# Attention, DFT mixing and feed-forward in one kernel: keys laid out per query tile, totals in bf16, the DFT tail added from PSUM

## The chip, the core and the metric

One core of one Trainium2 chip runs the whole program. The metric is the time of one execution on the device in microseconds (us). Five engines work side by side, each through its own list of instructions in a fixed order: PE (TensorE, matrix products), DVE (VectorE), ACT (ScalarE), POOL (GpSimd) and SP, which here only starts DMAs. They wait for each other by semaphores. PE takes its operands from SBUF and leaves products in PSUM, of which the kernel uses banks of 512 fp32 columns.

## What is computed

```python
# x: 8 batches x (32 global + 512 local rows) x 512, made by attention:
s_g   = scale * q_g @ k_all.T ;  out_g = softmax(s_g) @ v_all          # global queries see all 544 keys
s_ll  = where(|i - j| <= 32, scale * q_l @ k_l.T, -1e9)                # local: a band of 65 keys
s_lg  = scale * q_l @ k_g.T                                            # and all 32 global keys
out_l = softmax([s_lg, s_ll]) @ [v_g; v_l]                             # 8 heads of 64
X = real(fft(fft(x, axis=rows), axis=columns));  u = x + X             # mixing
un = (u - mean) / sqrt(var + 1e-6)                                     # rows of u
out = u + relu(un @ w_ch1) @ w_ch2                                     # 512 -> 2048 -> 512
```

All inputs are fp32. The kernel holds every matrix operand as two fp16 parts (hi and lo) and sums three products, hi by hi, hi by lo, lo by hi.

## The kernel before

**Attention.** Heads are taken in 32 pairs, four per batch; a pair's two heads lie on the lower and upper 64 of the 128 rows, so that their matmuls use half the rows each. The 512 local queries of a pair make four tiles of 128, in an order (`row_order`, L79) chosen for the DFT; the keys are in an order of their own (`key_order`, L84): 15 local keys, the 32 global ones, then all the rest, 559 columns with the doubled 15. Tile j needs 192 consecutive columns from 128j on, and the global ones. `scores` (L610) does two tiles: for each it makes a 192-column product and then a second one, of 64 columns in tile 0 (which takes keys of the far end) and of the 32 global ones in tiles 1 to 3, each in three hi/lo products for two heads. `masked` (L626, DVE) adds the mask and finds the row maximum `nm`; `exps` (ACT) takes the exponential; `p_hi` (ACT) and `p_lo` (POOL, L648) split it into fp16 parts; `turn` transposes it by DMA; `values` (L659) multiplies by the values (`vN` in key order, `vB` a shifted copy made by `v_out`'s DMAs), and `norm` divides. `g_scores`, `g_max`, `g_exp`, `g_values` do the same for the global queries of two pairs at once, `g_scores` as one 512-column and one 32-column product.

**Scales.** So that fp16 parts suffice, arrays are scaled by powers of two taken from sums of squares: ACT's `sums` (L528) leaves one column of partial sums per array, and a matmul with a constant matrix (`total`, L463; `w_norm`, L445, for the weights) adds them over the 128 partitions and spreads the result. Constant `part` and sums are fp32. `z_total` serves two pairs, `dft_scale` a batch.

**Mixing and feed-forward.** Per batch, `d_even` and `d_odd` (DVE, POOL) fold rows of X, `d_first` and `d_second` (L914, L949) are the matrix products of the DFT, `d_add`, `d_addc` (L966, L975) add the results into X. The 32 global rows of a batch go through `d_tailsec` and then `d_as` (ACT, PSUM to `asm`) and `d_tadd` (DVE: two additions from `asm`, L986 and L987, and two multiply-adds from PSUM, L989). Layer norm (`l_bn` to `l_lo`, with `l_un` L1027 and `l_lo` L1037) makes the two fp16 parts of a chunk of 256 rows; `l_turn` transposes by DMA, for chunk 0 `l_flip` (PE) and `l_put` (L1057 on DVE, L1059 on ACT) do it. `f_first` (L1085, `ps<-uh,wh`) and `f_second` (L1104, `acc<-wh,h`) are the feed-forward of 13 chunks; four more are done in two pairs by a scheme with fewer products (L1236, L1303). The weights are scaled and split at the start (`w_lo`, L472, DVE: `wh`).

**The order.** No queue decides at run time. Class `Plan` (L157) gets every step as a job (`jobs_*`) with its engine, a declared duration in us, what it reads and writes, and in some cases a due time; `targets` spreads due times backwards, and `run` places the jobs one after another on each engine by what is ready and what is due first, using the declared durations, margins (`PEM`: extra time asked between an input and PE) and buffer rings. The result is each engine's fixed list. Feed-forward jobs come last in rank and fill PE's gaps. So a changed duration or constant can reorder anything.

Of the kernel before, what the change touches and what calls it, by code (L numbers as in the profile page):

```python
# [20 lines left out]
P = 128  # L21
# [28 lines left out]
L_HOLD = 77.65  # L50
QUEUE = 1.933
LOOK_BY = 31.266
LN, LN1, LN2 = 41.656, 17.202, 49.261
# [5 lines left out]
APER = 103.0  # L59
PL = 34.52  # L60
T_AT, T_PACE = 799.979, 10.217
BOOST = 34.224
BOOST0 = 82.708
# [12 lines left out]
KW = 576  # L76
# [7 lines left out]
def key_order():  # L84
    a = np.arange
    return np.concatenate([a(433, 448), a(32), a(32, 544)])


def shape_constants():
# [23 lines left out]
    q, key = row_order().reshape(4, P, 1), key_order()  # L113
    for n in range(4):
        k = np.full(192, 9999)
        k[:min(192, 559 - P * n)] = key[P * n:P * n + 192]
        g = np.full(32, -1)
        k = np.concatenate([k, key[384:448]]) if n == 0 else np.concatenate([k, g, g])
        if n == 0:
            k[15:47] = -1  # L120
        m[:, n] = np.where((k[None, :] < 0) | (np.abs(q[n] - k[None, :]) <= 32), 0, 0xF149)
# [190 lines left out]
class Kern:  # L312
    def __init__(self, tc, stack, ins, out):
# [9 lines left out]
        self.part = c.tile([P, P], F32, name="part")  # L323
        nc.gpsimd.memset(self.part, 2.0 ** -13)
        self.partb = c.tile([P, P], BF16, name="partb")
        nc.gpsimd.memset(self.partb, 2.0 ** -8)
        self.kT = [c.tile([P, 1152], F16, name=f"kT{i}") for i in range(NKB)]
# [6 lines left out]
        self.junk = c.tile([P, 640], F16, name="junk")  # L334
# [17 lines left out]
        self.pg = c.tile([P, 544], F32, name="pg")  # L352
# [10 lines left out]
        nc.vector.memset(self.pgr, 0.0)  # L363
        self.wb = ep(name="wb", bufs=1)
# [79 lines left out]
    def w_norm(self, k, c):  # L444
        self.nc.tensor.matmul(self.wl[k, c][:, P:P + 1], self.part, self.mx2[:, 4 * k + c:4 * k + c + 1], start=True, stop=True)  # L445
# [61 lines left out]
    def load(self, p):  # L507
        s = self.state(p)
        qk = self.p2.tile([P, SL + 559], F32, name="qk", bufs=3)
        s["q"], s["k"] = qk[:, 0:SL], qk[:, SL:]  # L510
        self.nc.sync.dma_start(qk, self.qk[s["b"], s["hp"]])
# [83 lines left out]
    def prep_hi(self, p, nm):  # L595
# [4 lines left out]
        else:  # L600
            t = [s["kT"][:, KW * a:KW * a + 559] for a in range(2)]
# [8 lines left out]
    def scores(self, i):  # L610
# [76 lines left out]
    def g_scores(self, g):  # L687
        nc, G = self.nc, self.G[g]
        G["sg"] = S = [self.bank(("bank", "Sg", g, o)) for o in range(2)]
        for m, (a, c) in enumerate(((0, 0), (0, 1), (1, 0))):  # L690
            for o in range(2):
                for i in range(2):
                    st = self.st[2 * g + i]
                    qg = self.g[st["b"]]["T"][:, a, st["hp"], 0:64]
                    k = st["kT"][:, KW * c + 527:KW * c + 559] if o else st["kT"][:, KW * c + 15:KW * c + 527]
                    nc.tensor.matmul(S[o][64 * i:64 * i + 64, 0:k.shape[1]], qg, k, start=m == 0, stop=m == 2)  # L696

    def g_max(self, g):
# [12 lines left out]
    def g_hi(self, g):
        self.nc.scalar.activation(self.pgr[:, 0, 15:559], self.pg, AF.Copy)

    def g_lo(self, g):
        self.nc.gpsimd.tensor_sub(self.pgr[:, 1, 15:559], self.pg, self.pgr[:, 0, 15:559])
# [5 lines left out]
    def g_values(self, g):  # L721
# [3 lines left out]
        for c in range(5):  # L725
            n = P if c < 4 else 64
# [250 lines left out]
    def d_as(self, b):  # L977
        d = self.D[b]
        d["asm"] = asm = self.p1.tile([P, NL], F32, name="asm")
        eo = lambda t: t.rearrange("p (o m) -> p o m", o=2)  # L980
        self.nc.scalar.activation(asm[96:P].rearrange("p (m o) -> p o m", o=2), eo(self.d_psum_of(b, 2, 0)[64:96, 0:NL]), AF.Copy, scale=self.dsc[b][1][64:96])
# [776 lines left out]
```

## Time and profile before

| | us |
|---|---|
| median of 3 runs (lowest, highest) | 1017.65 (1015.54, 1017.81) |
| the profiled execution, its own time | 1017.34 |
| its span (first to last recorded instruction) | 1015.5 |
| PE busy (share of the span) | 924.4 (91%) |
| DVE busy | 732.5 (72%) |
| ACT busy | 627.9 (62%) |
| POOL busy | 582.0 (57%) |

The profile is one execution. An engine is busy while one of its compute instructions runs; a matmul's recorded duration includes its way through the array, so that matmuls in a row overlap, and what one costs is read from the distance between starts. Idle time before an instruction is given with the instruction of another engine that ended it (its releaser). "Granted clock" is the share of PE's full clock (2.4 GHz) in a stretch; it is near 1 or at 0.5.

### The profile page before, as it was taken

The page shows a single profiled execution, that of the slowest core. Times are in us where ns is not written, and L with a number is a line of the kernel's source. Part 1 is how long each engine was busy: PE and PEld are TensorE (multiplying, and loading weights), DVE is VectorE, ACT ScalarE, POOL GpSimd, SP SyncE. Part 2 cuts the span into 40 slices and gives each one's busy share as a digit, 9 for nine tenths or more (in the row PEclk, how much of TensorE's full clock was granted, in tenths as well). Part 3 has the DMA queues.
Part 4 walks back from the last instruction along what each step waited for, and adds up shares of the span by engine and source line. Part 5 has one row for each costly group of instructions (what it writes and reads, how often), then busy time and mean ns, then how long its engine had stood idle before and what let it go on. Part 6 is the DMA issues. An engine that isn't in the chain of part 4 may idle for free.

```text
span 1015.5 us, 25506 instructions
## 1 busy us (share of the span) xinstructions
PE 924.4 (91%) x9864; PEld 653.2 (64%) x9864; DVE 732.5 (72%) x1912; ACT 627.9 (62%) x1361; POOL 582.0 (57%) x861
## 2 busy tenths in 40 slices
PE   2555589999999999999999999999999999999996
PEld 1344466766676667677777767777777766666663
DVE  3687898888858977895688788767865665854543
ACT  6996778976796678758685776764653344411210
POOL 5797378675595469558646864692664097920000
PEclk9655579999999999999999999999999999999998
DMA  9899359635675486458636562843371142201001
GB/s 365 278 223 197 126 118 167 105 109 105 130 152 103 83 146 141 113 96 147 156 77 131 104 161 57 151 101 80 59 131 22 25 94 48 48 1 43 1 1 42
DMA packets 225974, 112.62 MB, mean 111 GB/s; under 512 B 200860, under 2 KB 208444, under 8 KB 225852
## 3 DMA queue, kind: packets, MB, share of 16 engines
q1 hardware_dynamic: 225852, 110.99, 49.8%
q8 instruction: 77, 1.26, 0.5%
q14 instruction: 45, 0.37, 0.1%
HBM read 47.40 MB, written 9.44 MB: 56 GB/s over the span
## 4 chain that ended last, share of the span: by engine, by line
PE 73%; DVE 8%; ACT 2%; issue 1%; POOL 0%; DVEq 0%; ACTq 0%; POOLq 0%
PE ps L1085 23%; PE acc L1104 22%; PE bk L1236 7%; PE ps L1303 4%; PE acc L1303 4%; PE bk L624 3%; PE bk L669 2%; PE bk L672 2%; PE bk L949 1%; PE bk L914 1%; DVE pe L632 1%; PE bk L696 1%; DVE xt L986 1%; PE bk L732 1%; DVE h L1094 1%
## 5 line engine op out<-in xcount | busy, mean ns | idle before, releaser
L1104 PE MATMUL acc<-wh,h 128*128 128x512 f16 x1248 | 287.5, 380 | 5.5 <-DVE h L1094 3.4
L1085 PE MATMUL ps<-uh,wh 128*128 128x256 f16 x2496 | 291.9, 274 | 0.2 <-DVE h L1094 0.2
L1085 PEld LDWEIGHTS <-wh 128*128 128x128 f16 x2496 | 241.5, 99 | 35.9 <-issue 0.9
L1104 PEld LDWEIGHTS <-h 128*128 128x128 f16 x1248 | 117.6, 98 | 133.8 <-DVE h L1094 4.3
L648 POOL TENSOR_TENSOR ph<-pe,ph 128x448 f16<-128x448 f32 (+1 forms) x128 | 141.6, 1116 | 75.8 <-ACT ph L643 57.4
L1094 DVE SCALAR_TENSOR_TENSOR h<-ps,h 128x512 f16<-128x512 f32 x104 | 71.6, 688 | 100.9 <-ACT h L1090 99.2
L1090 ACT ACTIVATE h<-ps 128x512 f16<-128x512 f32 x104 | 61.7, 594 | 117.6 <-PE ps L1085 114.8
L639 ACT ACTIVATE pe<-pe,nm 128x224 f32<-128x224 f32 (+1 forms) x256 | 107.0, 475 | 32.0 <-DVE nm L632 31.6
L632 DVE CUSTOM_DVE_ANT_0 pe<-bk,msk,z 128x224 f32<-128x224 f32 (+1 forms) x256 | 102.3, 453 | 10.3 <-PE bk L624 10.0
L643 ACT ACTIVATE ph<-pe 128x448 f16<-128x448 f32 (+1 forms) x128 | 72.8, 582 | 5.4 <-DMA pl<-ph 1.3
L669 PE MATMUL bk<-vN,pl 128*128 128x65 f16 x768 | 67.7, 200 | 5.7 <-DMA pl<-ph 5.5
L669 PEld LDWEIGHTS <-pl 128*128 128x128 f16 x768 | 59.3, 102 | 12.9 <-DMA pl<-ph 6.6
L624 PEld LDWEIGHTS <-qT 64*128 64x128 f16 x1536 | 51.1, 99 | 14.2 <-issue 10.8
L624 PE MATMUL bk<-kT,qT 64*128 64x192 f16 (+2 forms) x1536 | 57.9, 222 | 2.6 <-DVE X L685 0.8
L672 PEld LDWEIGHTS <-pl 96*128 96x128 f16 (+1 forms) x768 | 56.7, 102 | 4.4 <-issue 0.3
L1065 POOL TENSOR_TENSOR ve<-ve 128x2 f32<-128x2 f32 x17 | 9.4, 555 | 85.3 <-DVE unh L1037 35.0
L572 POOL TENSOR_TENSOR vf<-vf,z 128x640 f32<-128x640 f32 x32 | 41.6, 1300 | 28.7 <-DVE ge L534 14.7
L439 PE MATMUL wl<-wm 128*128 128x128 bf16 x128 | 18.2, 288 | 43.7 <-DVE wm L429 42.1
L583 POOL TENSOR_TENSOR vN<-vf,vN 128x640 f16<-128x640 f32 x32 | 45.4, 1417 | 13.1 <-ACT vN L579 12.8
L608 POOL TENSOR_TENSOR kT<-qk,kT 128x559 f16<-128x559 f32 x32 | 41.3, 1290 | 17.7 <-ACT kT L603 14.7
L672 PE MATMUL bk<-vB,pl 96*128 96x65 f16 (+1 forms) x576 | 51.2, 199 | 0.0
L1285 ACT ACTIVATE hb<-ph 128x512 f16<-128x512 f32 x16 | 10.1, 630 | 65.3 <-DVE ph L1270 65.3
(266 smaller groups left out, 1895.3 us busy)
## 6 DMA issues: line engine op xcount, KB each, us to landing
qk<-in_qk SPq DMA_DIRECT2D x32, 535.5 KB
rw<-in_moe_w_ch SPq DMA_DIRECT2D x22, 512.0 KB
vf<-in_v SPq DMA_DIRECT2D x32, 320.0 KB
out<-X SPq DMA_DIRECT2D x13, 512.0 KB
raw<-in_moe_w_ch SPq DMA_DIRECT2D x10, 512.0 KB
vB<-vN SPq DMA_DIRECT2D x32, 97.5 KB
vB<-vN SPq DMA_DIRECT2D x64, 32.5 KB
pl<-ph SPq DMA_TRANSPOSE x128
```

The costliest lines, as they stand in the source:

```text
L624: nc.tensor.matmul(S[h][:, t + w0:t + w1], qT[r, a, j], kT[r, k0:k0 + w1 - w0], start=m == 0, stop=m == 2)
L632: nc.vector.tensor_tensor_reduce(self.per[j][:, h, 0:w], S[h][:, t:t + w], self.msk[:, j, 0:w], z[:, 8:9], 3e38, op0=ALU.add, op1=ALU.min, ...
L639: self.nc.scalar.activation(pe[:, h], pe[:, h], AF.Exp, bias=nm[:, h:h + 1], scale=-1.0)
L643: self.nc.scalar.activation(ph[:, 0, :, 0:WIDE[i % 4]], self.per[i % 4][:, :, 0:WIDE[i % 4]], AF.Copy)
L648: self.nc.gpsimd.tensor_sub(ph[:, 1, :, 0:w], self.per[i % 4][:, :, 0:w], ph[:, 0, :, 0:w])
L669: nc.tensor.matmul(pv[:, j % 2, h], pl[:, 4 * a + 2 * h], vN[:, j, c, h, :], start=m == 0, stop=False)
L672: nc.tensor.matmul(pv[:, j % 2, h], pl[0:n, 4 * a + 2 * h + 1], vb, start=False, stop=m == 2)
L1085: nc.tensor.matmul(ps[:, q], wt[:, w, c0:c0 + P], uh[:, :, 4 * a + kt, :], start=n == 0, stop=n == 11)
L1094: self.nc.vector.scalar_tensor_tensor(h[:, 1], self.fps.pop((c, fp)), 0.0, h[:, 0], op0=ALU.max, op1=ALU.subtract)
L1104: nc.tensor.matmul(self.acc_f[c][j], h[:, a, q, j * P:(j + 1) * P], self.w[1, f][:, w, :], start=f == 0 and a == 0 and w == 0, stop=f == 1 ...
L1236: nc.tensor.matmul(ps, w[x], a[:, :, k * y + o + kt, :], start=m == 0, stop=m == 5)
L1303: nc.tensor.matmul(self.acc_f[c][j], h[:, a, q, j * P:(j + 1) * P], self.w[1, f][:, w, :], start=first and q + a + w == 0, stop=last and q ...
```

## The change

Keys. `key_order` repeats the 32 global keys in front of the key blocks: 655 columns in place of 559. From column 160j - 32 on (`key_at`), tiles 1 to 3 find the 32 global keys and their 192 local ones side by side, and `scores` makes one 224-column product of them; tile 0 keeps 192 + 64. The mask, the values' order (`vB` now has the global values in front, with four DMAs where there were three) and the global queries follow: `g_scores` skips the repeated columns with products of 113, 384 and 47 columns, 18 matmuls where there were 12. A pair's key load grows from 559 to 655 columns beside the 512 of q.

Totals. `total` and `w_norm` read the upper 16 bits of the fp32 sums as bf16, against a bf16 constant `parth`.

DFT tail. `d_as` and the two additions of `d_tadd` go; in their place `d_tadd` makes two more multiply-adds from PSUM.

Plan. Most declared durations and constants are replaced by other numbers; the feed-forward's products are the same.

```diff
 def key_order():
     a = np.arange
-    return np.concatenate([a(433, 448), a(32), a(32, 544)])
+    g = a(32)
+    return np.concatenate([a(433, 448), g, a(32, 241), g, a(241, 369), g, a(369, 497), g, a(497, 544)])
+
+def key_at(j):
+    return 160 * j - 32 if j else 0
...
-PEM, PEM0, SPM = 0.737, 0.718, 0.205
+PEM, PEM0, SPM = 0.944, 0.753, 0.179
...
     def w_norm(self, k, c):
-        ... self.part, self.mx2[:, 4 * k + c:4 * k + c + 1], start=True, stop=True)
+        ... self.parth, self.upper(self.mx2[:, 4 * k + c:4 * k + c + 1]), start=True, stop=True)
...
+    def upper(self, a):
+        return a.bitcast(BF16).rearrange("p (n t) -> p n t", t=2)[:, :, 1]
+
     def total(self, a, o):
         pb = self.bank(o)[:, 0:a.shape[1]]
-        self.nc.tensor.matmul(pb, self.part, a, start=True, stop=True)
+        self.nc.tensor.matmul(pb, self.parth, self.upper(a), start=True, stop=True)
...
-        nc.sync.dma_start(vB[0:64], vN[0:64, 1:4])
-        nc.sync.dma_start(vB[64:96, 1:3], vN[64:96, 4:5].to_broadcast([SG, 2, 2, 2, 65]))
+        nc.sync.dma_start(vB[32:96, 1:3], vN[0:64, 2:4])
+        nc.sync.dma_start(vB[0:32, 1:3], vN[0:32, 4:5].to_broadcast([SG, 2, 2, 2, 65]))
+        nc.sync.dma_start(vB[0:64, 0], vN[0:64, 1])
         nc.sync.dma_start(vB[64:P, 0], vN[0:64, 3])
...
     def scores(...):
-            for o in range(2):
+            for k0, w0, w1 in ((key_at(j), 0, 224),) if j else ((0, 0, 192), (key_at(3), 192, 256)):
                 for m, (a, c) in enumerate(((0, 0), (0, 1), (1, 0))):
-                    k0 = KW * c + (P * j, 384 if j == 0 else 15)[o]
-                    w0, w1 = ((0, 192), (192, WIDE[j]))[o]
                     for h in range(2):
                         r = slice(64 * h, 64 * h + 64)
-                        nc.tensor.matmul(S[h][:, t + w0:t + w1], qT[r, a, j], kT[r, k0:k0 + w1 - w0], start=m == 0, stop=m == 2)
+                        nc.tensor.matmul(S[h][:, t + w0:t + w1], qT[r, a, j], kT[r, KW * c + k0:KW * c + k0 + w1 - w0], start=m == 0, stop=m == 2)
...
     def g_scores(self, g):
-        for m, (a, c) in enumerate(((0, 0), (0, 1), (1, 0))):
-            for o in range(2):
+        for o, at, n in ((0, 0, 113), (0, 113, 384), (1, 0, 47)):
+            for m, (a, c) in enumerate(((0, 0), (0, 1), (1, 0))):
...
-    def d_as(self, b):
-        d = self.D[b]
-        d["asm"] = asm = self.p1.tile([P, NL], F32, name="asm")
-        ...  # ACT copies the even and odd halves out of PSUM
     def d_tadd(self, b):
-        ve, d = self.nc.vector, self.D[b]
-        x, a = d["xt"][96:P], d["asm"][96:P]
-        ve.tensor_add(x[:, 0:256], x[:, 0:256], a[:, 0:256])
-        ve.tensor_add(x[:, 511:255:-1], x[:, 511:255:-1], a[:, 1:257])
-        for (v, t), c in zip(self.pieces(x, self.d_psum_of(b, 2, 1)[96:P]), (self.dsc[b][4], self.dsc[b][3])):
-            ve.scalar_tensor_tensor(v, t, c[96:P], v, op0=ALU.mult, op1=ALU.add)
+        _, inv, _, c0, c1 = self.dsc[b]
+        x, ps = self.D[b]["xt"][96:P], self.d_psum_of(b, 2, 1)
+        for r, k in ((64, (inv, inv)), (96, (c1, c0))):
+            for (v, t), c in zip(self.pieces(x, ps[r:r + 32]), k):
+                self.nc.vector.scalar_tensor_tensor(v, t, c[96:P], v, op0=ALU.mult, op1=ALU.add)
...
-            add("PE", .25, self.z_total, g, r=[acc], w=[zt], margin=PEM if b else PEM0)
+            add("PE", .1, self.z_total, g, r=[acc], w=[zt], margin=PEM if b else PEM0)
...
-            add("PE", rate * .76, self.scores, 2 * p + h, ...)
+            add("PE", rate * (.61 if h else .65), self.scores, 2 * p + h, ...)
...
-                add("ACT", .42, self.d_as, b, r=[pb[0], dsc], w=[("asm", b)], **late)
-                add("DVE", 1.85, self.d_tadd, b, r=[pb[0], dsc, ("asm", b)], w=[("xta", b)], k=[xt], **late)
+                add("DVE", 1.60, self.d_tadd, b, r=[pb[0], dsc], w=[("xta", b)], k=[xt], **late)
```

What this moves on the engines' lists is shown at three places. A row is a line of the code, the instruction, what it writes and reads and its shape; an x and a number at the end stand for that many in a row.

On PE, inside the first score block of pair 4 (the first pair of batch 1): the end of a tile's wide products and the beginning of what follows. `bk_...` are the two PSUM banks of the two heads, kT and qT the keys and queries. The kernel before:

```order
L624 LDWEIGHTS qT
L624 MATMUL bk_123<-kT_63,qT 128x192
L624 LDWEIGHTS qT
L624 MATMUL bk_125<-kT_63,qT 128x192
L624 LDWEIGHTS qT
L624 MATMUL bk_123<-kT_63,qT 128x32
L624 LDWEIGHTS qT
L624 MATMUL bk_125<-kT_63,qT 128x32
```

The changed kernel, at the end of tile 0 and the beginning of tile 1:

```order
L632 LDWEIGHTS qT
L632 MATMUL bk_122<-kT_61,qT 128x64
L632 LDWEIGHTS qT
L632 MATMUL bk_124<-kT_61,qT 128x64
L632 LDWEIGHTS qT
L632 MATMUL bk_122<-kT_61,qT 128x224
L632 LDWEIGHTS qT
L632 MATMUL bk_124<-kT_61,qT 128x224
```

Before, every tile ends with matmuls of 32 columns (64 in tile 0); in the changed kernel tile 1 is 224-column matmuls alone.

On DVE, at the end of batch 0's attention: L429 and L435 work on the weights, L685 and L693 end a pair's `norm`, L831 and L841 begin `d_even`, L632 and L640 are `masked` (one row for the masked block, one for the row maximum). The kernel before:

```order
L684 RECIPROCAL dn<-dn 128x4
L685 TENSOR_TENSOR X<-bk_125,dn 128x2x128
L429 SCALAR_TENSOR_TENSOR wm<-ps_1269,lw 128x512
L831 TENSOR_TENSOR e_1307<-X 128x4x127
L832 COPY e_1307<-X 128x4
L835 TENSOR_TENSOR e_1307<-e_1307 128x2x128
L836 TENSOR_TENSOR e_1307<-e_1307 128x128
L837 TENSOR_TENSOR e_1307<-e_1307 128x128
L632 ISA pe,nm<-bk_122,msk,z 128x224
L632 ISA nm 128x1
L632 ISA pe,nm<-bk_123,msk,z 128x224
L632 ISA nm 128x1
```

The changed kernel:

```order
L640 ISA nm 128x1
L640 ISA pe,nm<-bk_124,msk,z 128x224
L640 ISA nm 128x1
L691 TENSOR_SCALAR dn<-bk_123,z 128x4
L692 RECIPROCAL dn<-dn 128x4
L693 TENSOR_TENSOR X<-bk_123,dn 128x2x128
L481 SCALAR_TENSOR_TENSOR wh<-wm,wsc,wh 128x512
L750 TENSOR_SCALAR dng<-bk_122,z 128x1
L751 RECIPROCAL dng<-dng 128x1
L752 TENSOR_SCALAR xg<-bk_122,dng 128x64
L435 SCALAR_TENSOR_TENSOR wm<-ps_1246,lw 128x512
L841 TENSOR_TENSOR e_1281<-X 128x4x127
```

Before, the first half of `d_even` (five rows) stands ahead of the last two masked units of the batch; in the changed kernel the masked units, the norm and the global rows come first.

On DVE again, between `l_lo` and `l_put` of chunk 0, the last steps ahead of the first feed-forward matmul; L975 and L985 are `d_addc`, L966 and L976 `d_add`, L1057 and L1060 `l_put`. The kernel before:

```order
L1037 TENSOR_TENSOR unh<-un,unh 128x512 x2
L975 SCALAR_TENSOR_TENSOR X<-bk_123,dsc,X 128x2x128 x4
L1057 COPY uh<-bk_125 128x512
L966 SCALAR_TENSOR_TENSOR X<-bk_124,dsc,X 128x2x128 x2
L1057 COPY uh<-flt 128x512
L966 SCALAR_TENSOR_TENSOR X<-bk_124,dsc,X 128x2x128 x2
```

The changed kernel:

```order
L1040 TENSOR_TENSOR unh<-un,unh 128x512 x2
L640 ISA pe,nm<-bk_122,msk,z 128x256
L640 ISA nm 128x1
L640 ISA pe,nm<-bk_124,msk,z 128x256
L640 ISA nm 128x1
L640 ISA pe,nm<-bk_122,msk,z 128x224
L640 ISA nm 128x1
L640 ISA pe,nm<-bk_124,msk,z 128x224
L640 ISA nm 128x1
L985 SCALAR_TENSOR_TENSOR X<-bk_121,dsc,X 128x2x128 x4
L976 SCALAR_TENSOR_TENSOR X<-bk_123,dsc,X 128x2x128 x2
L1060 COPY uh<-bk_122 128x512
```

Four masked blocks of pair 4 now stand between the two, and the bank that `l_put` reads is the one that two of them have read.

## Rows read from the trace of the kernel before

**Rows 1.** What PE waited for, 175 to 1015 us: total, times, longest.

```profile
PE acc L1104 <- DVE h L1094: 3.4, 2, 1.8
PE bk L914 <- DVE z L934: 1.7, 1, 1.7
PE bk L463 <- ACT junk L528: 1.4, 1, 1.4
PE bk L624 <- DVE nm L632: 0.8, 1, 0.8
...
PE bk L463 <- DVE xt L989: 0.5, 1, 0.5
```

**Rows 2.** PE's timeline, 118 to 140 us: start, duration, instruction, count [idle before].

```profile
133.92 4.87 PE L1085 MATMUL ps<-uh,wh 128*128 128x256 f16 x24
```

**Rows 3.** PE's timeline, 454.5 to 461.3 us.

```profile
455.01 2.75 PE L1104 MATMUL acc<-wh,h 128*128 128x512 f16 x12
457.60 2.78 PE L1085 MATMUL ps<-uh,wh 128*128 128x256 f16 x24
460.31 0.82 PE L624 MATMUL bk<-kT,qT 64*128 64x192 f16 x24
461.06 0.20 PE L669 MATMUL bk<-vN,pl 128*128 128x65 f16 x1
461.10 0.20 PE L672 MATMUL bk<-vB,pl 96*128 96x65 f16 x1
```

**Rows 4.** PE's timeline entered inside that score block, at its thirteenth matmul.

```profile
460.65 0.48 PE L624 MATMUL bk<-kT,qT 64*128 64x192 f16 x12
```

**Rows 5.** PE's timeline, 440 to 466 us, in the DFT's second product.

```profile
446.83 0.23 PE L951 MATMUL bk<-altr,zr 64*32 64x129 f16 x1
446.99 0.53 PE L949 MATMUL bk<-c2r,z 128*32 128x129 f16 x9
```

**Rows 6.** PE's timeline, 594.8 to 595.4 us: totals and the next work.

```profile
594.92 0.28 PE L463 MATMUL bk<-vax,part 128*128 128x7 f32 x2
...
595.28 0.38 PE L1085 MATMUL ps<-uh,wh 128*128 128x256 f16 x2
```

**Rows 7.** `d_tadd` by line: durations in ns (least/median/most), first and last start.

```profile
L986 DVE TENSOR_TENSOR xt<-xt,asm x8: 421/422/4840, 146.3 to 802.5; 32x256 f32<-32x256 f32 x8
...
L989 DVE SCALAR_TENSOR_TENSOR xt<-bk,dsc,xt x16: 483/490/495, 147.1 to 803.7; 32x256 f32<-32x256 f32 x16
```

**Rows 8.** Timelines of DVE, POOL and ACT, 264 to 278 us.

```profile
266.60 4.84 DVE L986 TENSOR_TENSOR xt<-xt,asm 32x256 f32<-32x256 f32 x1
...
269.01 2.14 POOL L648 TENSOR_TENSOR ph<-pe,ph 128x512 f16<-128x512 f32 x2
...
273.24 0.85 ACT L639 ACTIVATE pe<-pe,nm 128x224 f32<-128x224 f32 x2 [3.61 <-DVE nm L632]
```

**Rows 9.** PE by stretch: window, length, busy (matmuls), granted clock, DMA share, GB/s.

```profile
367.00:370.00 3.00, 3.00 (x32) 0.50 1.07 230
```

**Rows 10.** PE's timeline, 358 to 373 us.

```profile
366.50 1.73 PE L624 MATMUL bk<-kT,qT 64*128 64x192 f16 x24 [0.78 <-DVE nm L632]
368.16 3.82 PE L1085 MATMUL ps<-uh,wh 128*128 128x256 f16 x24
```

**Rows 11.** Timelines of DVE and ACT, 88 to 136 us.

```profile
88.53 0.69 DVE L831 TENSOR_TENSOR e<-X 128x508 f32<-128x508 f32 x1 [0.98 <-DMA X<-xd]
...
129.31 1.33 DVE L1037 TENSOR_TENSOR unh<-un,unh 128x512 f16<-128x512 f32 x2
...
133.28 0.41 DVE L1057 COPY uh<-flt 128x512 f16<-128x512 f16 x1
...
92.97 0.85 ACT L639 ACTIVATE pe<-pe,nm 128x224 f32<-128x224 f32 x2 [4.00 <-DVE nm L632]
...
108.46 0.74 ACT L528 ACTIVATE junk<-vf 128x640 f16<-128x640 f32 x1 [0.55 <-DMA vf<-in_v]
```

**Rows 12.** DVE's timeline, 166 to 173 us.

```profile
166.66 4.99 DVE L472 SCALAR_TENSOR_TENSOR wh<-wm,wsc,wh 128x512 f16<-128x512 f32 x2
```

More of the change, by code (lines that the diff above doesn't have):

```diff
@@ L75 @@
 AT = (0, 256, 0, 224)
-KW = 576
+KW = 672
+NKC = 655
 def row_order():
@@ L113, in shape_constants @@
     q, key = row_order().reshape(4, P, 1), key_order()
+    key = np.where(key < 32, -1, key)
     for n in range(4):
[L115 to L118, printed above, removed]
+        k = np.full(256, 9999)
+        w = 192 if n == 0 else 224
+        v = key[key_at(n):key_at(n) + w]
+        k[:len(v)] = v
         if n == 0:
-            k[15:47] = -1
+            k[192:] = key[key_at(3):key_at(3) + 64]
         m[:, n] = np.where((k[None, :] < 0) | (np.abs(q[n] - k[None, :]) <= 32), 0, 0xF149)
@@ L322, in __init__ @@
         self.consts = ins
[L323 to L327, printed above, removed]
+        self.parth = c.tile([P, P], BF16, name="parth")
+        nc.gpsimd.memset(self.parth, 2.0 ** -13)
+        self.kT = [c.tile([P, 2 * KW], F16, name=f"kT{i}") for i in range(NKB)]
         vN = self.vna = c.tile([P, 2, 1300], F16, name="vN")
@@ L444, in w_norm @@
     def w_norm(self, k, c):
-        self.nc.tensor.matmul(self.wl[k, c][:, P:P + 1], self.part, self.mx2[:, 4 * k + c:4 * k + c + 1], start=True, stop=True)
+        self.nc.tensor.matmul(self.wl[k, c][:, P:P + 1], self.parth, self.upper(self.mx2[:, 4 * k + c:4 * k + c + 1]), start=True, stop=True)
     def w_scale(self, k, c):
@@ L600, in prep_hi @@
         else:
-            t = [s["kT"][:, KW * a:KW * a + 559] for a in range(2)]
+            t = [s["kT"][:, KW * a:KW * a + NKC] for a in range(2)]
         s["n" + nm] = t
@@ L1369, in jobs_pair @@
         hold = L_HOLD if b else 0.0
-        add("SP", .44, self.load, p, w=[qk], svc=1.6, hold=hold, queue=QUEUE if p else None)
-        add("SP", .44, self.load_v, p, w=[vf], svc=1.0, hold=hold, queue=QUEUE if p else None)
+        add("SP", .47, self.load, p, w=[qk], svc=1.6, hold=hold, queue=QUEUE if p else None)
+        add("SP", .56, self.load_v, p, w=[vf], svc=1.0, hold=hold, queue=QUEUE if p else None)
         add("ACT", .72, self.sums, p, "q", r=[qk], w=[acc, q], margin=LDM)
-        add("ACT", .75, self.sums, p, "k", r=[qk], w=[acc, k], margin=LDM)
+        add("ACT", .83, self.sums, p, "k", r=[qk], w=[acc, k], margin=LDM)
         add("ACT", .83, self.sums_v, p, r=[vf], w=[acc], margin=LDM)
@@ L1396, in jobs_scores @@
         for nm, o, d in (("k", k, kT), ("q", q, qT)):
[L1397 to L1399 removed]
+            x = .05 if nm == "k" else 0
+            add("ACT", .63 + x, self.prep_mul, p, nm, r=[z, o, qk], w=[o])
+            add("ACT", .53 + x, self.prep_hi, p, nm, r=[o, qk], w=[d])
+            add("POOL", 1.20 + 3 * x, self.prep_lo, p, nm, r=[o, qk, d], w=[d])
         vN, vB = ("vN", p), ("vB", p)
@@ L1408, in half @@
             S = [("bank", "S", 2 * p + h, o) for o in range(2)]
-            add("PE", rate * .76, self.scores, 2 * p + h, r=[kT, qT], w=S + [("pe", 4 * p + 2 * h + n) for n in range(2)], t=U[2 * h], margin=pem)
+            add("PE", rate * (.61 if h else .65), self.scores, 2 * p + h, r=[kT, qT], w=S + [("pe", 4 * p + 2 * h + n) for n in range(2)], t=U[2 * h], margin=pem)
             for n in range(2):
@@ L1412, in half @@
                 pe, ph = ("pe", u), ("ph", u)
-                add("DVE", .92 if p < 8 else .84, self.masked, u, r=[*S, z, ("msk",), pe], w=[pe, ("nm", u)])
+                add("DVE", .80, self.masked, u, r=[*S, z, ("msk",), pe], w=[pe, ("nm", u)])
                 add("ACT", .77, self.exps, u, r=[pe, ("nm", u)], w=[pe])
@@ L1425, in vals @@
             first = [X] if hp + h == 0 else []
-            add("DVE", .84, self.norm, i, r=[pv, z], w=([xM] if h else [xA, xD]) + first, k=[X])
+            add("DVE", .82, self.norm, i, r=[pv, z], w=([xM] if h else [xA, xD]) + first, k=[X])
         half(0)
@@ L1634, in jobs_duo @@
             b = prod(s, "P1", t)
-            add("ACT", .36, self.p_copy, u, s, "P1", r=[b, *end, ("xtf", 15) if s < 5 else ("asm", 7)], w=[x1] + (own if u == 0 and s in (5, 7) else []), k=own, t=-1e3, back=False)
+            add("ACT", .36, self.p_copy, u, s, "P1", r=[b, *end, ("xtf", 15) if s < 5 else ("xta", 7)], w=[x1] + (own if u == 0 and s in (5, 7) else []), k=own, t=-1e3, back=False)
             b = prod(s, "P2", t)
```

134 lines of the change are left out of this document (66 added, 68 removed).

## The prediction

> **What bounds the kernel now.** The profiled execution took 1017.34 us: a span of 1015.5 and 1.84 around it. The median of the runs shown is 1017.65, so one sum serves both. The first view is the list of what TensorE (PE) waited for. From 175 us to the end it holds six waits, five of them in [rows 1], 7.8 us together, in 840 us; the rest is matmul after matmul. So from there on the time falls only by what PE no longer streams, and by those waits. Before that PE is mostly idle: the start is a chain through DVE, ACT and the weight loads, and ends with chunk 0's first feed-forward matmul at 133.92 [rows 2]. An edit counts in full if it shortens PE's own stream after 133.92, removes one of the waits, or moves 133.92; otherwise not at all.
>
> **Score tiles.** Of a pair's four tiles three lose their 32-column matmuls, six per tile, and their 192-column ones become 224 wide. Streaming rate: twelve 512-column matmuls run from 455.01 to 457.60 [rows 3], 0.216 each, 0.42 ns a column. The two heads' matmuls lie on separate row halves and overlap: twelve (six steps) of 192 and of 32 columns take from 460.31 to 460.65, the twelve behind them start there [rows 3, 4]. A 192-column step is 192 x 0.42 = 0.081, three are 0.243, so three 32-column steps are about 0.34 - 0.243 = 0.09, some 0.028 each: twice what their 32 columns stream. A 224-column step is 0.0945, 0.0135 more. Saving per step 0.028 - 0.0135 = 0.0145, per tile 0.044. After 133.92 the static order has 55 of 64 score blocks, 27.5 pairs: 27.5 x 3 x 0.044 = **3.6**; I take 3.5. The ends: zero, if a short step costs only its columns, and 7.2, if the declared durations of a block (0.76 before, 0.65 and 0.61 now) were the chip's: (0.11 + 0.15) x 27.5. The latter needs the time in which PE empties between matmuls on half its rows and full ones to shrink too. It is there: the 129-column matmul on 64 rows holds the next one off from 446.83 to 446.99 [rows 5], 0.16, of which 129 x 0.42 = 0.054 streams. Nothing in the edit touches that, so I stay at the step arithmetic. The global queries' scores stream the same 544 columns in 18 matmuls in place of 12; 16 pairs of heads, a few hundredths each, 0 to 0.3 lost: inside the rounding.
>
> **Totals.** A total is an fp32 matmul of 6 or 7 columns, which the trace shows as two matmuls. Two totals in a row hold the next work off from 594.92 to 595.28 [rows 6]: 0.18 each. In bf16 a total is one pass. No row shows that; the nearest is a 65-column matmul on 128 rows among its like, 461.06 to 461.10 [rows 3], 0.04. So a total falls from 0.18 to somewhere between 0.03 and, if the first of a kind still pays for its weights, 0.09: 0.09 to 0.15 saved. Of the program's 24 totals 20 stand after 133.92: 1.8 to 3.0, and I take **3.0**, since ordinary weight loads hide behind the previous matmul everywhere else. The three power-of-two scale steps that read a total on DVE are unchanged.
>
> **The DFT tail.** Two SBUF additions on 32 partitions (L986, L987) and ACT's copy (L981) go; two fused multiply-adds from PSUM come. L986 takes 422 ns in the median but 4840 at worst; the PSUM form L989 lies at 483 to 495 in all 16 [rows 7]. So normally the tail costs DVE about 0.14 more, under PE's stream, hidden by DVE's slack. But two of the eight are long, the 4.84 at 266.60 [rows 8] and one in batch 2, and both reach PE. At the first DVE stands still while POOL runs four instructions without a gap, the last two at 269.01 (1.07 each, ending at 271.15) [rows 8]. ACT is then 3.61 late with the softmax [rows 8], comes late to its sums, and PE's total waits 1.4 for them [rows 1]. The second costs PE 0.5 before a total and 0.8 before the scores [rows 1], and the granted clock falls to 0.50 between 367 and 370 [rows 9], the 1.2 GHz level: the score block takes 1.73 instead of 0.82, the 24 first-layer matmuls 3.82 instead of 2.78 [rows 3, 10]. Sum 1.4 + 0.5 + 0.8 + 0.9 + 1.0 = **4.6**, all gone if an operand from PSUM keeps DVE clear of POOL, as sixteen of sixteen did.
>
> What the Trainium skill states on this ("SBUF — State Buffer", Who interferes with whom) is that a DVE instruction with two SBUF inputs contends with a GpSimd instruction that reads SBUF, that one with a single SBUF input does not, and that the loser is blocked for the whole of the other's instruction. Our rows agree on which form waits, but not on how long: by the page DVE would lose one POOL instruction, 1.07 to 1.35 us, PE would hardly have noticed, and this part would be worth nearly nothing; the row says 4.84 across four, and I go by the row.
>
> **The start.** The order moves two things. In batch 0, DVE did d_even's first half ahead of the last two masked units: it waited 0.98 for its data, worked from 88.53, and ACT waited 4.00 for the row maxima behind it [rows 11]. Now the masked units stand ahead of d_even: up to 0.98 + 4.00 = 5.0 less on that chain. In exchange two masked units of pair 4 (four DVE instructions, 1.6) and the tail of the mixing now stand between l_lo and l_put of chunk 0, on DVE, and PE has pair 4's scores and the total of pairs 4 and 5 ahead of the flip, in a bank that the flip needs back. Before, l_lo ended at 130.64 and the last l_put ran from 133.28 to 133.69 [rows 11], 3.05 later. Now 1.6 + 1.7 + 0.9 + 0.4 + some 1.2 of bank and flip make 5.8: 2.7 lost. Net **2.3 gained**; the ends are 5 gained, if the flip finds its bank free, and 5 lost, if the 5.0 are caught by the weight loads and the total keeps the flip waiting.
>
> **What is off the path.** The k array is 96 columns longer, so ACT and POOL take 0.05 to 0.22 more on each of some 130 instructions, about 7 us on each over the run; ACT and POOL are idle for a third of it. The key loads grow by 48 KB each and one small DMA per pair is added on SP. All this costs nothing while the scores of a pair are issued ahead of need; if POOL is the last to arrive, 0.2 at each of 27 pairs is 5.4, and that is in the upper end.
>
> **Sum.** 1017.34 - 3.5 - 3.0 - 4.6 - 2.3 = 1003.9. The other waits of [rows 1] stay in (3.4 and 1.7), as the new order gives no row for them to go. Forecast **1004.5**, half a microsecond above for the extra work on SP and POOL. Its own range, by the bounds of each term, is 1000 to 1009.
>
> **Rivals.** (A) *The stall moves.* DVE keeps instructions with two SBUF inputs: the weights' L472, two of which took 4.99 at 166.66 while POOL worked [rows 12], d_even's additions, the layer norm's root. With a new order they meet POOL's row of p_lo, v_lo and prep_lo in other places. Then only the streamed terms are left, and 0.3 of the start: 1017.34 - 6.5 = 1010.8. For it: POOL is fuller than before. Against it: in the 840 us only two such meetings reached PE, though L472 and d_even met POOL often. The page named above gives the same: by its rule the remaining two-input instructions contend as before. (B) *The streamed terms are larger*: the declared block durations hold, 7.2 for 3.5, and the waits 3.4 and 1.7 go as well, because PE's units are ordered further behind their inputs: 1004.5 - 3.7 - 4 = 997. Against it: the rows on the emptying of PE. (C) *Slower, by the start.* PE runs in order, so the total of pairs 4 and 5 ahead of chunk 0's DFT and flip makes the whole feed-forward wait for ACT's sums of pairs 4 and 5, whose values come by DMA; before, ACT met them when it had time. The price is one for one: each microsecond that 133.92 moves is one of the end. It decides from 133.92 - 2.3 + 14 on, since 11 are gained elsewhere: first feed-forward matmul later than about 148. For it: ACT's queue is in order and ht stands behind those sums. Against it: in before ACT's sum over the first of those values ran at 108.46 after 0.55 of waiting for its load [rows 11], 25 us ahead of 133.92. It gives 1021 and more. (D) *The change doesn't do what it says*: short steps cost only their columns, the first bf16 total still pays for its weights, and a new wait takes the rest: 1014.6 to 1020.
>
> **How the numbers follow.** Forecast 0.42 (1000 to 1009); A 0.25 (1007 to 1014.5); B 0.12 (993 to 1000); D 0.11; C 0.10. A measurement of this kernel can tell 0.3% from no change, 3.05 us: 1014.6 to 1020.7. Faster is forecast, A and B: 0.79. Same is D, 0.11. Slower is C, 0.10. The range leaves out C, most of D and the far half of B, 0.2 together: 996 to 1015.
>
> **What would show it.** Scores right: a second half's block in PE's timeline goes from 0.75 to about 0.66 between first matmul and the next work; 0.60 speaks for B. Totals right: next matmul 0.03 to 0.05 after a total. Tail right: no instruction of d_tadd over 0.6 us, and no PE wait that leads to it; a PE wait that leads to L472, d_even or the layer norm speaks for A. Start right: first feed-forward matmul between 129 and 134; beyond 148, C. The prediction is wrong if PE's waits after 175 us come to more than about 8 us in a kernel whose d_tadd is never long, or if the first feed-forward matmul moves by more than 5.

## The result, and the profile after

The changed kernel takes 1000.92 us (median, 1000.05 to 1001.96) where before took 1016.6 in the same comparison: ratio 0.9847, 95% interval 0.9828 to 0.9866, some 15.7 us less. The forecast was 1004.5, range 996 to 1015. The profiled execution took 1000.05 (span 998.1), 17.3 less than that of before. So direction and range held. But the sum held by luck: two of its steps were wrong in opposite directions. The start came later where it was forecast earlier, and the waits that were left in the sum went away.

The waits of PE from 175 us to the end, 8.5 us in the kernel before (five of the six stand in [rows 1]), are one in the kernel after (total, times, longest):

```profile
PE acc L1306 <- DVE h L1293: 0.2, 1, 0.2
```

The same by stretch (window, length, busy and matmuls, granted clock, DMA share, GB/s), before:

```profile
200.00:300.00 100.00, 97.94 (x1143) 1.00 0.61 123
300.00:400.00 100.00, 97.05 (x1151) 0.98 0.62 120
400.00:500.00 100.00, 98.30 (x1146) 1.00 0.63 132
500.00:600.00 100.00, 98.19 (x1160) 1.00 0.52 109
```

and after:

```profile
200.00:300.00 100.00, 100.00 (x1152) 1.00 0.61 125
300.00:400.00 100.00, 100.00 (x1112) 1.00 0.59 124
400.00:500.00 100.00, 100.00 (x1097) 1.00 0.60 121
500.00:600.00 100.00, 100.00 (x1108) 1.00 0.59 125
```

The 1.7 to 3.0 us of idle in every hundred are gone; in these 400 us PE does not stop once, and the clock is full.

The first feed-forward matmul, at 133.92 before [rows 2], in PE's timeline after:

```profile
135.19 1.01 PE L1055 MATMUL bk<-idnr,unh 128*128 128x128 f16 x8 [7.06 <-DVE nm L640]
...
139.11 0.37 PE L1088 MATMUL ps<-uh,wh 128*128 128x256 f16 x1 [0.51 <-ACT uh L1062]
139.74 4.29 PE L1088 MATMUL ps<-uh,wh 128*128 128x256 f16 x23 [0.26 <-DVE uh L1060]
```

It comes 5.2 later. PE's flip (L1055) has waited 7.06, at the end for a masked block of pair 4, whose bank it takes. The steps of [rows 11] on DVE after (`d_even`'s second half, l_lo, the last l_put):

```profile
105.84 0.85 DVE L841 TENSOR_TENSOR e<-X 128x512 f32<-128x512 f32 x1 [0.20 <-DVE X L693]
...
132.62 1.33 DVE L1040 TENSOR_TENSOR unh<-un,unh 128x512 f16<-128x512 f32 x2
...
139.27 0.42 DVE L1060 COPY uh<-flt 128x512 f16<-128x512 f16 x1
```

The streamed terms after, each with the work that follows it: a second-half and a first-half score block, the global queries' values, and a total in bf16:

```profile
143.97 0.75 PE L632 MATMUL bk<-kT,qT 64*128 64x224 f16 x12
144.65 0.61 PE L1088 MATMUL ps<-uh,wh 128*128 128x256 f16 x4
...
370.23 0.80 PE L632 MATMUL bk<-kT,qT 64*128 64x192 f16 x18
370.96 1.25 PE L1107 MATMUL acc<-wh,h 128*128 128x512 f16 x5
...
448.48 0.66 PE L742 MATMUL bk<-vN,plg 128*32 128x65 f16 x60
449.07 2.79 PE L1088 MATMUL ps<-uh,wh 128*128 128x256 f16 x24
...
466.37 0.18 PE L472 MATMUL bk<-vac,parth 128*128 128x7 bf16 x1
466.41 3.76 PE L1088 MATMUL ps<-uh,wh 128*128 128x256 f16 x33
```

From start to next start a second-half block is 0.68 and a first-half one 0.73, where both were 0.75 [rows 3]; a total is 0.04 where two took 0.36 [rows 6]. And `d_tadd`, by line, which answers to [rows 7]:

```profile
L992 DVE SCALAR_TENSOR_TENSOR xt<-bk,dsc,xt x32: 477/486/495, 150.3 to 799.4; 32x256 f32<-32x256 f32 x32
```

None is long. The table adds up the distances between PE's starts by function, from the first feed-forward matmul to the last matmul, in us of each profile. The time until the next start counts for a function, so waits and slow clock are in it. `order_only` is an experiment below.

| | before | order_only | after |
|---|---|---|---|
| first feed-forward matmul at | 133.9 | 134.7 | 139.1 |
| from there to the last matmul's start | 871.7 | 857.0 | 849.0 |
| f_first and f_second | 558.7 | 549.4 | 548.9 |
| scores | 43.6 | 41.1 | 38.4 |
| totals | 4.7 | 3.5 | 0.6 |
| values of the local, of the global queries | 47.0, 9.7 | 45.5, 9.8 | 45.5, 8.2 |
| d_first and d_second | 39.9 | 39.2 | 39.2 |

22.6 us less from there on (871.7 to 849.0) and a start 5.2 later make the 17.3.

### The profile page after: what moved, and what is told of

The parts are those of the page before. It is cut to its first block, busy times and chain, and to the rows that moved or that the text cites. A ratio compares the mean times of both kernels' runs of the same rounds, so it can differ in the third digit from the quotient of the medians.

```text
span 998.1 us, 24488 instructions
## 1 busy us (share of the span) xinstructions
PE 906.3 (91%) x9352; PEld 631.3 (63%) x9352; DVE 725.2 (73%) x1913; ACT 632.0 (63%) x1353; POOL 584.9 (59%) x860
## 4 chain that ended last, share of the span: by engine, by line
PE 84%; ACT 4%; DMA 4%; DVE 3%; POOL 2%; issue 1%; SPq 1%; DVEq 0%; POOLq 0%; ACTq 0%
PE ps L1088 28%; PE acc L1107 27%; PE bk L1239 7%; PE ps L1306 4%; PE acc L1306 4%; PE bk L632 4%; PE bk L677 2%; PE bk L680 2%; PE bk L959 2%; DMA rw<-in_moe_w_ch 2%; PE bk L924 1%; DMA vf<-in_v 1%; PE bk L706 1%; ACT junk L537 1%; PE bk L742 1%
## 5 line engine op out<-in xcount | busy, mean ns | idle before, releaser
L640 DVE CUSTOM_DVE_ANT_0 pe<-bk,msk,z 128x224 f32<-128x224 f32 (+1 forms) x256 | 101.9, 454 | 12.7 <-PE bk L632 10.4
L677 PE MATMUL bk<-vN,pl 128*128 128x65 f16 x768 | 64.9, 199 | 7.0 <-DMA pl<-ph 7.0
L618 POOL TENSOR_TENSOR kT<-qk,kT 128x655 f16<-128x655 f32 x32 | 46.3, 1447 | 24.0 <-ACT kT L613 20.7
L632 PE MATMUL bk<-kT,qT 64*128 64x224 f16 (+2 forms) x960 | 53.4, 255 | 0.3 <-DVE nm L640 0.3
L603 ACT ACTIVATE qk<-qk,z 128x655 f32<-128x655 f32 x64 | 46.5, 768 | 0.7 <-DVE z L543 0.7
L537 ACT ACTIVATE junk<-qk 128x512 f16<-128x512 f32 x64 | 43.9, 686 | 3.6 <-DMA qk<-in_qk 2.3
```

Of the source, the lines that this page charges most:

```text
L640: nc.vector.tensor_tensor_reduce(self.per[j][:, h, 0:w], S[h][:, t:t + w], self.msk[:, j, 0:w], z[:, 8:9], 3e38, op0=ALU.add, op1=ALU.min, ...
L677: nc.tensor.matmul(pv[:, j % 2, h], pl[:, 4 * a + 2 * h], vN[:, j, c, h, :], start=m == 0, stop=False)
```

## The experiments

Two questions: which part brought what, and why the start came late. The theory was that the edits and the order add up. The rivals: the order alone removes the waits, or the edits alone do.

**totals.** The order of the kernel before, with bf16 totals:

```diff
-        self.nc.tensor.matmul(pb, self.part, a, start=True, stop=True)
+        self.nc.tensor.matmul(pb, self.parth, self.upper(a), start=True, stop=True)
```

> The kernel before with the bf16 totals alone; every engine's order stays. Theory: a total takes PE 0.03 us instead of about 0.22, as the changed kernel's trace has it; 20 of them stand after the first feed-forward matmul, so 3.5 to 3.8 us less, 1013.5 where before is 1017.3. Rival: what PE gains here it loses again in the waits on DVE that follow in the same order (8.5 us of them stay), and less than 2 us arrive.

Measured: 1015.94, ratio 0.9979 (0.9966 to 0.9992), 2.1 less. The totals themselves fall from 4.7 to 1.9 us on PE, as the theory has it; but PE's waits after 175 us grew from 8.5 to 10.7:

```profile
PE acc L1107 <- DVE h L1097: 5.0, 2, 3.2
PE bk L917 <- DVE z L937: 1.7, 1, 1.7
PE bk L466 <- DVE nm L635: 1.3, 1, 1.3
PE bk L627 <- DVE nm L635: 1.1, 1, 1.1
```

The wait on h is 5.0 where it was 3.4. Behind the longer of these waits the granted clock is at its lower level, 1.2 GHz, for 6 us; in the kernel before it was full there:

```profile
586.00:592.00 6.00, 5.59 (x17) 0.50 0.41 123
```

So in this profile nothing of the gain arrives behind the start: from the first feed-forward matmul to the last matmul it takes 872.3, before 871.7. Its first feed-forward matmul, at 131.6, is 2.3 earlier than in the profile before, and batch 1's first load is issued 2.5 earlier, in the same lists; why is not known. By time the theory's 3.5 lies at the interval's end (0.8 to 3.5 less) and the rival's "less than 2" inside it; the trace speaks for the rival.

**tail.** The order of before, `d_tadd` from PSUM; ACT's copy stays as dead work so that no list changes:

```diff
     def d_tadd(self, b):
...
-        ve.tensor_add(x[:, 0:256], x[:, 0:256], a[:, 0:256])
-        ve.tensor_add(x[:, 511:255:-1], x[:, 511:255:-1], a[:, 1:257])
-        for (v, t), c in zip(self.pieces(x, ...[96:P]), ...): ve.scalar_tensor_tensor(...)
...
+        for r, k in ((64, (inv, inv)), (96, (c1, c0))):
+            for (v, t), c in zip(self.pieces(x, ps[r:r + 32]), k): ...scalar_tensor_tensor(...)
```

> The kernel before with d_tadd alone changed (four multiply-adds from PSUM); ACT's copy stays as dead work, so that every engine's order stays. Theory: no instruction of d_tadd is longer than 0.6 us, PE's waits of 1.4, 0.8 and 0.5 us and the stretch at the 1.2 GHz level behind them are gone: 4.6 us less, 1012.7. Rival (another DVE instruction with two SBUF inputs, or the POOL row itself, takes the place of the long one): the waits stay within 1 us of what they were, 1016 to 1017.

Measured: 1013.67, ratio 0.996 (0.9944 to 0.9976), 4.1 less: the 4.6 hold within the interval (2.4 to 5.7). DVE's timeline at the two places of the long additions, and what is left of PE's waits:

```profile
265.08 1.82 DVE L988 SCALAR_TENSOR_TENSOR xt<-bk,dsc,xt 32x256 f32<-32x256 f32 x4
...
356.44 1.82 DVE L988 SCALAR_TENSOR_TENSOR xt<-bk,dsc,xt 32x256 f32<-32x256 f32 x4
```

```profile
PE acc L1103 <- DVE h L1093: 4.4, 2, 3.0
PE bk L914 <- DVE z L934: 1.9, 1, 1.9
PE bk L914 <- DVE nm L632: 0.7, 1, 0.7
```

Four instructions in 1.82 where one took 4.84 [rows 8]; the waits of 1.4, 0.8 and 0.5 are gone, and with them the slow stretch of [rows 9]. The others stay; the one on h is 4.4 where it was 3.4, and behind it the granted clock is 0.59 from 585 to 588.

**edits.** All three edits with the old constants and declared durations, ACT's copy kept as dead work (into a scratch tile):

```diff
-STEP = 5.317 ... BOOST0 = 70.998, every declared duration of the changed kernel
+STEP = 5.316 ... BOOST0 = 82.708, every declared duration of the kernel before
```

> All three code edits (keys, totals, tail) in the order of the kernel before: the old constants and declared durations, ACT's copy kept as dead work. Theory: streamed work less by 2.6 (scores), 3.7 (totals) and 1.5 (the global queries' value products, 0.1 each), and 4.6 for the tail: 12.4 less, 1005, with the waits of 3.4, 1.7 and 0.7 on DVE still there and the first feed-forward matmul near 134. Rival (the edits alone bring the whole, the new order nothing): 1000 to 1001.

Measured: 1012.59, ratio 0.9951 (0.9934 to 0.9968): 5.0 less, not 12.4. Both theories fall. The profiled execution is one of the slowest of the eight (1015.58; they go from 1010.1 to 1016.2), so it can show where the gain went, but not how much in the median. The streamed terms shrank as they should (scores 43.6 to 38.6, totals 4.7 to 0.8, global values 9.7 to 8.2), and the waits came to 9.8, more than they had been:

```profile
PE acc L1113 <- DVE h L1103: 3.8, 2, 3.0
PE bk L924 <- DVE z L944: 2.1, 1, 2.1
PE bk L924 <- DVE nm L640: 1.1, 2, 0.7
PE bk L677 <- DMA pl<-ph: 1.1, 2, 0.7
PE bk L677 <- DVE X L693: 1.0, 1, 1.0
```

Behind the two longest waits, on z and on h, the clock is at its lower level, where in the kernel before it was full:

```profile
416.00:419.00 3.00, 3.00 (x9) 0.50 0.13 22
590.00:593.00 3.00, 3.00 (x12) 0.50 0.29 76
```

With waits and slow clock, `f_first` and `f_second` took 564.3 where they had taken 558.7. The first feed-forward matmul came at 135.9, 1.9 later than in the kernel before.

**order_only.** The changed kernel's constants and declared durations with the old code; the additions from SBUF read a tile of zeros in place of ACT's copy:

```diff
+        self.nc.vector.tensor_add(x[:, 0:256], x[:, 0:256], a[:, 0:256])
+        self.nc.vector.tensor_add(x[:, 511:255:-1], x[:, 511:255:-1], a[:, 1:257])
```

(and the key and totals edits undone)

> The order of the changed kernel (its constants and declared durations) with the code of before: 559 key columns, fp32 totals, and d_tadd with two additions from SBUF; in these the even part of the 32 global rows' DFT is left out (zeros are added). Theory: the new order removes the waits of 3.4, 1.7, 0.7 and 2.2 us on DVE and the slow clock behind them, 10 us in all, and its start costs 5: 1012, if no long addition falls on PE's path; the first feed-forward matmul comes near 139. Rival (the waits went because of the edits): 8 us of waits stay and the start's 5 come on top, 1022.

Measured: 1004.42, ratio 0.9872 (0.9856 to 0.9888), 13.0 less, more than any edit and than the 5 expected. PE's only wait after 175 us, and the first of the two additions by line:

```profile
PE acc L1297 <- DVE h L1284: 0.2, 1, 0.2
```

```profile
L980 DVE TENSOR_TENSOR xt<-xt,asm x8: 422/430/1351, 146.5 to 801.5; 32x256 f32<-32x256 f32 x8
```

So the order by itself removes every wait of more than 0.2 us after 175 us, those of the DFT tail among them: with it the additions from SBUF take 1.35 us at most and hold up nobody. This run also leaves out ACT's copy, as the changed kernel does; how much of the 13.0 comes from that is not tested. By the difference of the ratios the edits bring 2.5 to 3.6 of the changed kernel's 15.6 to 16.6 us (its two measurements, above and below); each ratio is uncertain by 1.6 to 1.9 us.

**old_keys.** The changed kernel with the key edit undone (559 columns, 192 + 32, 64 rows in the last global value product), same order:

```diff
-            for k0, w0, w1 in ((key_at(j), 0, 224),) if j else ((0, 0, 192), (key_at(3), 192, 256)):
+            for o in range(2):
...
+                    w0, w1 = ((0, 192), (192, WIDE[j]))[o]
```

> The changed kernel without its key edit: 559 key columns, 192 + 32 column score products and 64 rows in the last value product of the global queries, with the changed kernel's order, bf16 totals and tail. Theory (the longer key loads and preparations delay the start by what the trace of order_only lacks): the first feed-forward matmul comes near 135 instead of 139.3, 4.2 us earlier, and PE's work after it grows by 2.7 in the scores and 1.6 in the global value products, 4.3: 1000, as the changed kernel. Rival (the key edit costs nothing at the start): the first feed-forward matmul stays near 139 and the time is 1004.5.

Measured: 1001.87, ratio 0.9857 (0.9837 to 0.9876): beside the changed kernel's 0.9847, the same within the intervals. In PE's timeline:

```profile
135.95 0.37 PE L1079 MATMUL ps<-uh,wh 128*128 128x256 f16 x1 [0.44 <-ACT uh L1053]
136.58 5.06 PE L1079 MATMUL ps<-uh,wh 128*128 128x256 f16 x23 [0.25 <-DVE uh L1051]
```

The start is 3.2 earlier than after's 139.11, and from there to the end PE needs 854.3, 5.2 more. The theory holds in kind: of what the key edit gives on PE (2.7 in the scores and 1.6 in the global values of it), it loses the greater part at the start.

**first8, first4.** The changed kernel with the old layout of keys for the first eight, or four, pairs:

```diff
...
+            if p < OLD:
+                parts = ((P * j, 0, 128), (15, 128, 160), (P * j + 128, 160, 224)) if j else ((0, 0, 192), (384, 192, 256))
```

(and 559 columns in their load and preparation)

> The changed kernel, but the first eight pairs (batches 0 and 1) load and prepare 559 key columns in the old order, and make the score tiles 1 to 3 from three products of 128, 32 and 64 columns; all other pairs as changed. Theory: the start is that of old_keys, 4 us earlier, and pairs 4 to 7 pay about 1.2 us more on PE: 997. Rival (the start is set by something else): 1001 to 1002, first feed-forward matmul near 139.

> As first8, but only for the first four pairs (batch 0). Theory: of the 4.2 us at the start 1.5 to 2 come from the first loads and batch 0's preparations and about 2 from the loads of batch 1 behind them; so 998 here, with the first feed-forward matmul near 137. Rival (all of it comes from batch 0): 996 and 135.

Measured: first8 998.54, ratio 0.9828 (0.981 to 0.9847); first4 999.57, ratio 0.9844 (0.9826 to 0.9863). The medians are 2.4 and 1.4 us below the changed kernel's, the intervals overlap. First feed-forward matmuls: 137.5 for both, for first8

```profile
137.53 0.27 PE L1099 MATMUL ps<-uh,wh 128*128 128x256 f16 x1 [0.44 <-ACT uh L1073]
```

so not 135. 1.6 of the delay goes (2.9 against the second profile of the changed kernel, below), the rest stays. In the profiles four pairs do as much as eight. Neither version is shown to beat the changed kernel.

**after_again, v3, v3_first8.** v3 takes the fourth DMA of `v_out` away from SP:

```diff
-        nc.sync.dma_start(vB[0:32, 1:3], vN[0:32, 4:5].to_broadcast([SG, 2, 2, 2, 65]))
+        nc.gpsimd.tensor_copy(vB[0:32, 1:3], vN[0:32, 4:5].to_broadcast([SG, 2, 2, 2, 65]))
```

> The changed kernel once more, beside the two below: 1000 to 1002, no PE wait over 0.5 us between 175 us and the end, first feed-forward matmul 4 to 6 us later than in the kernel before (139 within 1).

> The changed kernel with three DMAs in v_out as before: the copy of the global values into vB (32 rows) is made by POOL. Theory (at the start SP's list is the late one: the four issues of v_out take 3.3 to 4 us on SP where three took 2.2, and the loads of batch 1 stand behind them): the loads of batch 1 are issued 1 to 1.7 us earlier, the first feed-forward matmul comes near 138, and the time is 999.5. Rival (the longer key loads and preparations alone are late): no change, 1001, or 0.5 more for POOL's copies.

> v3 and first8 together: three DMAs in v_out, and 559 key columns for the first eight pairs. Theory (keys and the fourth DMA together make the start late): first feed-forward matmul within 1 us of old_keys' 136.2 and 997 to 997.5, 1 less than first8. Rival (they overlap): as first8, 998.5.

Measured: after_again 1000.78 (0.9837, 0.9821 to 0.9853), v3 1000.65 (0.9834, 0.9817 to 0.985), v3_first8 999.37 (0.9827, 0.9809 to 0.9845); first feed-forward matmuls at 140.4, 139.9 and 138.0. The rival holds: the first of batch 1's loads is issued at 99.5 in v3, 0.5 and 1.6 earlier than in the two profiles of the changed kernel, but the start is not earlier. SP's fourth issue is not what makes it late.

**long_load.** old_keys with only the loads lengthened to 655 columns:

```diff
-        qk = self.p2.tile([P, SL + 559], F32, name="qk", bufs=3)
-        s["q"], s["k"] = qk[:, 0:SL], qk[:, SL:]
+        qk = self.p2.tile([P, SL + 655], F32, name="qk", bufs=3)
+        s["q"], s["k"] = qk[:, 0:SL], qk[:, SL:SL + 559]
```

> old_keys with the longer loads alone: every pair's load brings 655 key columns (583.5 KB), of which the last 96 are used by nothing; sums, preparations and scores stay at 559. Theory A (the loads make the start late): first feed-forward matmul 138 to 139 where old_keys had 136.2, and 1003.5 where it had 1001.9. Theory B (ACT's and POOL's longer preparations and the score tiles of the first batches do): 136 to 137 and 1001.9.

Measured: 1003.91, ratio 0.9864 (0.9836 to 0.9891), old_keys 0.9857: no difference to tell. The median is where theory A had it, but the kernel before was 1.2 slower in this comparison too, so the times do not decide. The profile's first feed-forward matmul is at 136.4, old_keys' at 136.0: theory B, in one trace each. By these the longer loads alone do not make the start late. What does is then the rest of the key layout in the first batches: the longer sums and preparations on ACT and POOL, the order of the values and the products beside them. Which of these is not separated; first8, which shortens loads, sums and preparations but makes three products per tile, takes back 1.6 to 2.9 of the 3 to 6 (see the start, below).

**gv96.** One number of the kernel before:

```diff
-            n = P if c < 4 else 64
+            n = P if c < 4 else 96
```

> The kernel before with one number changed: the last value product of the global queries takes 96 rows (32 of them zeros times values) instead of 64. Theory (a product on half the rows makes PE empty its array before and after): each block of 60 such matmuls takes 0.59 instead of 0.69 us, as in the changed kernel, with the same 65 columns streamed. Rival (the 0.1 came from elsewhere): 0.69 stays.

PE's timeline, the kernel before and then gv96, the same block with the same neighbour:

```profile
356.70 0.76 PE L732 MATMUL bk<-vN,plg 128*32 128x65 f16 x60
357.39 0.35 PE L949 MATMUL bk<-c2r,z 128*32 128x129 f16 x3
```

```profile
358.37 0.66 PE L732 MATMUL bk<-vN,plg 128*32 128x65 f16 x60
358.86 0.34 PE L949 MATMUL bk<-c2r,z 128*32 128x129 f16 x3
```

0.69 becomes 0.49 here, more than elsewhere; the median of 14 blocks goes from 0.694 to 0.590, the sum from 9.7 to 8.3. More rows, less time: the theory's number holds. That PE empties its array there is the reading of it; the rows show the time alone. One time, 1018.41, says nothing on the whole.

## Why the prediction was right, and where it was not

**What bounds the kernel.** Right: PE's stream, its waits with the slow clock behind them and the first feed-forward matmul account for the 17.3.

**Score tiles, 3.5.** Right in kind, a little too large: 2.7 (41.1 to 38.4 with the order held fixed). The half blocks went from 0.75 to 0.68 and 0.73, where the same steps give 0.66 and 0.71. So a step saves a little less than the 0.0145 of the sum; which of its two prices is off is not shown. The blocks stay far above the declared 0.61 and 0.65, and rival B's 7.2 fell.

**Not in the sum: global values, 1.6.** The edit raised the last product of the global queries from 64 to 96 rows. The prediction used the very row that prices this, a 64-row product among full ones [rows 5], for the scores alone, and did not look for other products on half the rows.

**Totals, 3.0.** Right: 2.9 with the order held fixed, and a total lands at the low end of its bounds (0.03 to 0.04). In the old order the time fell by 2.1, but the profile of `totals` shows its gain of 2.8 eaten by waits and slow clock.

**The DFT tail, 4.6.** Right as a mechanism and in size, in the order that the trace showed: 4.1. But in the changed kernel the order had already taken those waits away, so the edit itself is worth nothing that the traces show there. The Trainium skill's rule ("SBUF — State Buffer", Who interferes with whom), by which a DVE instruction with two SBUF inputs contends with a GpSimd instruction that reads SBUF, fits the form of the instructions in both orders. A wait of about one POOL instruction fits the 1.35 us in `order_only` and not the 4.84 across four [rows 8]. Why one wait ends after an instruction of POOL and the other does not is not shown.

**The start, 2.3 gained.** Wrong: 5.2 lost, 6.5 in the second profile of the changed kernel. A move of more than 5 is what the prediction itself had named as a sign of being wrong, and 5 lost was the end of its range. Two steps failed. First, the 5.0 of `d_even` did not reach the path: in both kernels DVE starts the second half of `d_even` when the batch's last norm is done, at 105.58 before and 105.84 after. With the old keys the new order does bring it forward, to 101.90 in `order_only` and 104.15 in `old_keys` (the old order has 103.7 to 105.7 in five profiles); with the new keys that is gone. The cost of the other step was right: from the end of l_lo (133.95) to the end of the last l_put (139.69) it is 5.7 where 5.8 was forecast, and 3.05 stood before. Second, "all this costs nothing" was said of the longer key preparations, from shares of the whole run.

What carries the start is in the chain that ended last: the load of batch 1's values, then ACT's sums of pairs 4 and 5, and behind them in ACT's list `ht` and `eh`, which chunk 0's DFT needs. It is the chain of rival C. The first load of batch 1 in SP's list, in `order_only` and in the changed kernel, and the load of the values in the latter's chain:

```profile
95.37 0.57 SPq L511 DMA_DIRECT2D qk<-in_qk  x1
```

```profile
100.00 0.57 SPq L520 DMA_DIRECT2D qk<-in_qk  x1
...
102.56 5.76 DMA vf<-in_v
```

In the nine profiles of the new order the first feed-forward matmul follows that first load by 38.1 to 40.4 us; in the five of the old order by 32.8 to 34.7. So the order costs about 6 behind the load and, with the old keys, issues it earlier (95.4 to 98.3, where the old order with them has 98.5 to 101.0). In the two profiles of the changed kernel it is issued at 100.0 and 101.1, and 5.2 and 6.5 are lost. By the profiles the key layout costs 2 to 4 us at the start in the old order (135.9 against 131.6 to 133.9) and 3 to 6 in the new one (139.1 and 140.4 against 134.7, 136.0 and 136.4 with the old layout). What in the key layout holds SP up is not shown.

**The other waits stay.** Wrong, and the largest step: the waits of 3.4 and 1.7 stayed in the sum, "as the new order gives no row for them to go", and with them, unnamed, one of 0.7 and the 2.2 on wh before 175 us. They went with the order alone. The new plan declares some of DVE's steps longer (`d_even` 3.25 for 2.95, `d_odd1` 1.7 for 1.3) and asks for more margin before PE; `order_only` shows that constants and durations together do it by the order they make, not which of them.

**The rivals.** A fell: nothing takes the stall's place, though DVE's additions with both inputs in SBUF are still long in places, as `d_even`'s at 376 us:

```profile
376.34 2.60 DVE L846 TENSOR_TENSOR e<-e 128x128 f32<-128x128 f32 x1
```

PE does not wait behind them. B's second half (the waits go) came true, its first did not. C had the place right, not the price: PE's total of pairs 4 and 5 waits 6.99 for ACT's sums, ahead of chunk 0's DFT,

```profile
113.88 0.17 PE L472 MATMUL bk<-vac,parth 128*128 128x7 bf16 x1 [6.99 <-ACT junk L537]
```

and the start is 5 late, not 14. D did not occur.

## What to carry to other kernels

When PE runs through a fixed order at saturation, price edits as a sum only if PE's waits go too: in the old order work that was shorter by some 12 us gave 5, as PE waited longer for its producers and its clock was low behind some of the waits. Where a planner's numbers change with the code, run the two apart; here the numbers alone gave 13 of 16. And weigh "off the critical path" stage by stage: what ACT, POOL and the DMA issues did held up PE nowhere in the changed kernel after 175 us, and at the start it carried the path.

## What the runs showed of the hardware that was not expected

Among products on 128 rows a value product on 96 rows costs less than one on 64 at the same 65 columns: a block of 60 matmuls, 12 of which change, falls from 0.694 to 0.590 us (median). And a wait of PE can cost more than itself: in `edits` the granted clock was 0.50 for 3 us behind each of the two longest waits, in `totals` for 6 us behind one, where the kernel before had it full. The kernel before spread from 1013.9 to 1022.8 over 55 executions, the changed one, whose PE does not wait, from 1000.0 to 1002.0 over eight; that the stalls make the difference is not shown.
